# Regrouping the last rows of k and q for the first segment: through DRAM instead of by products with identity columns

## Chip, cores and metric

The kernel runs on one core of a Trainium2 chip. The metric is the device time of one execution in microseconds (us); the figure given for a kernel is the median of several runs. Beside it stands one profiled execution, whose trace shows every instruction of the engines: PE (TensorE, matrix products; PEld is its weight load), ACT (ScalarE), DVE (VectorE), POOL (GpSimd) and SP (SyncE, which here only issues DMAs).

## What is computed

Two layers, each an attention block with a memory and then a feed-forward block, on x of 2048 tokens by 640 in bf16:

```
x = x + A(layernorm(x)); x = x + B(layernorm(x))      # and the same once more
A:  q, k, v = x@wq, x@wk, x@wv           # 32 heads of width 20, 4 segments of 512 tokens
    for s in range(4):
        p     = softmax(q_s k_s^T * scale + causal mask)
        o_s   = g * (phi(q_s) M) / (phi(q_s) z) + (1 - g) * p v_s
        M, z += phi(k_s)^T v_s, sum(phi(k_s))          # phi(t) = t + 1 if t > 0 else exp(t)
    return o @ wo
B:  relu(x@w1) @ w2                                    # inner width 1728
```

## The kernel before

**Tiling.** Tokens go in 8 segment passes (2 layers `a` by 4 segments `s`), each of 4 tiles of 128 tokens. Per pass: layer norm (`ln1`), projections to k and q (`proj_kq`, products on L972) and to v (`proj_v`, L1017), the regrouping of k and q (`relay`), scores with exp and mask (`scores`, L1324, L1338, L1314), their product with v (`apply`, L1406), the memory's write and read (`mem_write`, L1187; `mem_read`, L1274), the output projection (L1598), and the feed-forward block (`ffn`, L1664 and L1696).

**The layout of k and q.** PE works on four heads at once, one in each 32-partition quarter. A head is 20 wide. The projection therefore gives 5 chunks `c` of 128 columns; in each quarter the rows 0 to 19 are one whole head and the rows 20 to 31 are 12 columns of the heads that are left over. So heads of the groups `g` = 0 to 4 can be used where they are (`kqA`), and the groups 5, 6, 7 lie scattered in the last 12 rows of the quarters of all five chunks. `relay` gathers them into `kqL` [128, 2, 3, 512]: k and q, three groups `m`, 20 rows in each quarter. There is one `kqL` buffer for all passes.

**Two ways to gather.** For the passes in `RELAY_PE`, which is pass 0 only, `relay_pe` (L1097 and on) does it on PE: DVE clears 128x896 elements of hT (L1104) and copies columns of the identity into it (7 copies, L1108), seven selection matrices; PE multiplies them with `kqA`, 7 products for k and 7 for q (L1130), and DVE or ACT moves the six results from PSUM to `kqL` (L1113, L1114). For the other passes `relay_dma` (L1054 and on) has SP issue four DMAs that write the leftover rows to a DRAM buffer `kq_scr` (L1067), one for each quarter, and four that read them back in the new grouping (L1080); read `r` waits for write `r`, and the first read waits for the `kqL` buffer. The reads fill 20 of the 32 rows of a quarter.

**Who needs kqL.** The scores of groups 5, 6, 7 (the second half of each pass's score rounds), the second half of the memory's write (a transposition by DMA, `ktok<-kqL`, L1169) and of its read (L1240, L1242).

**The order of work.** Nothing is ordered by hand. Each function is a stream of operations; a planner (`Sched`) simulates the engines with assumed costs and takes at each point the operation that can start first, ties by a due time. The due times are a packed table (`TABLE`), one entry for each operation. The planner's result is one fixed list of instructions for each engine, and every engine works its list in order. A wait for a semaphore at the head of a list therefore holds everything behind it on that engine. Where the planner foresees that PE is idle it puts products of the identity with itself there (L787), which nobody reads.

**Score rounds.** A pass has 4 pairs of head groups with 5 rounds each, 160 rounds in all; they are counted from 0 here. A round is one group of row-packed products (L1324) into four PSUM banks, X and Y of two banks each, and two exps of 1024 columns on ACT (L1335, L1338) that empty X and Y. There is only one X and one Y, so a round cannot begin before both exps of the round before are done.

Of the kernel before, what the change touches and what calls it, by code (L numbers as in the profile page):

```python
# [13 lines left out]
T = 2048  # L14
D = 640
# [399 lines left out]
c-n1R36PxCaqj<`nSW+>X7)a`yV_lyD+wJ)!srA^2nC57bA%g&v6En%!-WHJ2vANLTqGpeByk+u3Ak)0#*T>-n+lXU48g`6!2*dJBH0MtD<to-  # L415
+TH1V{rzwL9f50WXa3{8e%<~0_`2T=dh;YFS4mky*`@usUMx*gkOq7o))skR*N7(>8PRUZOG&<}H)2e$#Bu^=TqHj32IPNq0p4DOQ7xD|q#bzo
F}!J(Zuz!eg83JUYDoflTaUxsm3WuKT~X#@-
ZEUT2F)MpB8*&txv@mxXbS!pOBQe2<pZ6CcMEWx$C_nXj=39fH&q(tDP4`H%P}X1cLAvXP6zQFgL7Zz<LL^_4e>V{)Q*L0S-
hPMDp!NsoII$1Bv;7iF}7FE(Y10SB*=m8J$je)Vdg^oXD}m>=~!bSzT0F}7s@73+JrY{&}e}^ROjF-i&aC&RhC5<-
75#6xdE<Qz^5<osnJ}5F%cy_1<%*uNf#&|(q_nYw(QVRJwaa5UdlWNJMxlF1y`%V>lV2cn*7{>IdZuS%Bh&Y60}#!DmfF{x)2<%m*eCN{C`}Im  # L420
-F!KVm#X{)9}3zqff{4`53=I&Vdd#fci4I6!TWgXQf9@mYH%Rba^i%I8~NnPnUsGFXo*p*JJEC(D+GGkwx!s2DjtdggF`P&U#4k)Yxy-
Y$XfJ`3`p?gMBGLqB7((OPNsHAy4K8jd&W#I@zub(47wnV`w~!(Nn?SpnL}FuLFff>6BJJ&+|Kns|t98MnL^U*hruBgF-Xrbz(nk--
>us#P}w>?UhF$K^`O4Q~$GZH3hop!MG4}t7>~U4!do@{yithU~U7nGY_`jiE&dfvJclS;O{J0ZxK2?Pj0|$<F^3Gro$SF9NmP~m*Z&$94S1)$F
<o*1r!V5FvOS;Pks!KXp@~f4?c3dJgjHSZF&y&<WAiz-_r}_e9T@ZKhSBQ`m8R;+BfPK<xz}Z0~?qFKYd!~$}DJe8FU$dzS*{iRTe;>F>Sp;cI
z$j4NY{rM+ZRb=ekj@)9=fePUy#nM)h<0*R)8VR04e4E`^{Q;?Con0F;dO%Q_!-8MmwB>SOmj-
eujl&G1Oecb?}v+9BTr<kELkeb61&0-q$aJU2EO7sx?I3e~{zQg-Vk<92H&?^@-
ES{!)~mgv*QsyY*&UdoS2I0e$%T?F0}Sra;8y0+P6vzryvapc!s)u{QY&Q$%Bj#0Pg6~xT?`33xsz{*YLywkI-
P=wdm`^b&0*I3R`Ojb!g%aZKMkb0>mdl83BW`!mL$4A5~i&szaGbGnpzDX#SQ)!G+i8@K<+DzO1gd_V_jkpKC<K81})iB)+ua5s3$C*@ble!C>
mH2gYg1VVr9T#EBg@4p8*!ZlYQG24)Vwl>7UpFsKIr6CK(5(~Jt(Uw@WUS50lU~KyqvvF8!~gfB;G`JfxR}@bw4JMzQp@w5zH@alcq!-
pQQi{3X0vsc<~a}Xj*=x;_crm8_$c2=#@?@&r=v0-vgP_6O5}}G->qpgpq_#{E`y_dz+|43Be9M=RvJ}{_2!FJ{a4)t-  # L430
3@Dn(KW`qi2Mee5jv{&F5%{gR*4O&I;Iv|%z7Sot3=3)9{CJXFY|~38ek(e4^FgQ<1D6piA5;l;Sr69Hp~nDPxHLD-
Q1^U(RpVJH628$ABNy4N;O`;C#rsGLjkSiTD_+(=F~KtaFI{-=zS>KWf6;OUTfK}s>9Bj6Rk&_mv@mjgzq=YFZ6ExDbYjXg-Kk=xcxAlS~iO%$
!ig?PmIw;JU^GYIOF2v1htUt_@KN>3k>SwU&K|j={{#DwXIWC%lJhnT@nMcN7-
(eM#f2Lb06{LpiY0uK2FBYth@`Ks@earHabd~l(Ok1axtyqY(+KkM8D3eeV0YNRJz)Zj;Ue98OStt9Yd~~Ej2p|MHekPkU>5Ad8^~uG;U~SLNl
q%ReD3jT@75e*$ICB6WLvnb05%4X@{N2R@;D)F9F{V>K^bsKr6R34Rt?<wGQhH?BAQZ0%&2qynrViz+!(1tsB1mIV^Wn6TQxnFX+WirbvDu7m(
9`({BJ-
{7nB&p3pAfr04W`ptZMvE?VS8JxTr^IHFnpO#cMDd=WNsJy7Zea+UrI5Xr@w>`XykgRYBM?Jn7>kAsiXFzRKwS$`t$;QkR^3FPm~GvN3ZJozLj
P3SS0m4}QOd=CQI+yG>GraqyMK|?2k*3-HQX!Z?YohsJZ1wAy$m2$6MEvtbsmH|)g#Iqda-
347Pk#7Q#&zI*h_I{m>t9_by`cL(AVC!C>vcJ%4Py_hTNC}yKJJvd^H_NXyki@3fK$~~ye*Kl)4m<L(-
vjbr`X%URv24?KfgHvWffi#g{$2l+sPr_@zDXX?-Jn0N>rlnKp&dE`bk+*Xp9UOQhNb4@AN5MevQ>`<ZXDK-sBfE^XZ@8_t2bkA1NQD?u(6jk@  # L440
z=NXT=@$0)($=kpw%h+p}k|BhrJ5yVm>^ENZ2ELb*E0jPM#0c`k;Oal01Q`;{{c{O>f8DFMtilq3a#c`7YFHuj~7I1gk#`JzanuUoN)iIY!t#E
DSphdw2tJ`8TL0M(IbFK+37unWgf5)Eu3_RTi}#ghed}eFX;Vf~Gy}{{rrphuvwDSM(I<X^SQ?D?=pbgT`ZOaqJ+q;De_SRmqF`kbVOGqsR-
>G5Q)vFbCRu6?*>z_{P)Nt0(mtVA%lDSnc)-
<S>6P;kpm_`yJ>Z03JS1*2?4hvK|5wJ_xQo;Ho^Tkq1C&CUoax#$h1iS9A%auY!x0bqIS?1P=k8EX9oJ*nz{a6GIptQP?i*k%w&l&#<!}=_jG3
0j%gjjyyE+0yr=`58*BQIir=|kM6Y!BMSu9gBa2WZM4f}m@|xhvnV?c`6+`Oa|V383I7XOA6R5*g9ok_TXPw>ErUjc@iSNtSq0I8+Gr|9l_5<t
Yo2D==apI6lrbWU=Zo+;?B($$%TY0&&&K<z*8~YI@@KJcuR_iRGCWjp88L7<EO4khNORij@Ki5FhoQqg0Vs`Y*3HehsApsHE>4bs|G-
7qnArOa%zTBlkHzZ9eeTeHmnrsWk=~o+fv2fitC9|A4H<-xKI3p*m}Y(7;k+8E2^}Ju>yU*ZuLvv8f@hyi^ifJPaey7MXx#1O4%6IVk-
7vgw5qIumC^xN_Ct&u0c>K2nuUZen`G14VF~8M#N8pDn*A3U!EKeS6zR=16qhBI^-
!<9L5a%DJ*Jh|W&T=5EWl6WpouFO<w6}E@uc0w_);BKNos}3yMXtTHC^bCQO;qZz|}e)>}xM1_^~(FWoG{)$i0R-
BbTEi?m$$BA+ssAu1DDk66+#94eBtGC+~P!x7K8>k!0=2VLU&T#dEc0eVveX*HQXelfUdRy&<6@rGSTeE1b=E%;Y1Q<?ghl`M;`@n#&@BZ&l;H  # L450
s+klC#dW&18C%%jn9u}=WQd#+>-
hSR)v}j?&N?|6UVlEUXDL3<#s5LXq}ve*=YflzV~yk@MBJ#td(0*R#Ns^UC=;LhuC~jHS;97=YX$EO)ct#i=rL<mU$)@=y|^pT{#QvqX5NbUU!
-j<p-
%1tVr*xeXhQaF06I98bj*e~g2!oy7qg&;Cibxk)MuIXi230Tpcm_}l;wxueL14hLSV}r<7UozmT9cWew}p+R^jTcAP>DX%BQObv9n)?=G)~$tk
6!K<!P6O*cO4t2EPw9rpdmlX<(3uZYm>BVwr){)*|qEv0s#9;Uh<?ZH&h;?aVlthlrO)PB9u4%q+-
xen0r>m#3={Y0bj(3Z5T_nA<4d(u=@v8~(a5^J@o3by&o^#Q&=Qr1zwE{b(Q?pn*K)8zi4!!oBTJ9=!fBR=<h&){R<;b-U$R-
K<}xr*+5z@Hri;ty1fL?M2SE$XK9fM(ib8Cn%sjZ1AloRRlr`Q)wIMJBBWkn&0$s3|2nVudtW3QrnzI7C0l%{VY&-
t(dXe#`~ReGcx!IYF0d^&Ge59$C^bovO=)_YKNTVH-
K(IHi6$f?LSL9NcK6R=M|A*XMx7AfkGF8!@H1UU(z4x1+<m_M#c9Ca>#VCd}%iQhVGNwfM2&k+eh@bz)@>~VNOAYP4dT;au4!uH*H}Bvfo<pc^
2{iebT@0{_y1BcK^@)Z~51Gd*l;CKKIr9qJ=ZIsr3tABjTOQoYgKZE{4CRH&Mq~7qd;?9Am<#J=6YS4W0evV40@xOW9YPDdtICuF^O8ujE=|>_  # L460
8<^Iq5n5%nu~7jtKs08DJyp(Qh(uHL#j7EoQjevE1UtcsiGIx6uklfWflzhj`nIOkx@2Y*uuC!_06Md5gK0p@1T6FviSVnf*qPv8=0P+W4&eFZ
S%<fk0kjW?9TNHUkA$;I}cXAp?&L=qY9&OR;xL@z%z65^s3yhBshj3p><}SnDvbRRiPi!=N+8b$t4un*e$?-
cH0=I}NbjW}e;Fj2KtbL9Yvu?Oge#w~_tPHq0zypPS%|y_nqt4tm+wEfP26sPPur=;e7rPz2(ze(_v6fjTxVcHq8@=Uue*l6*$K2Cc0{)GRWlM
D*nzM6?*y&~DUBqwMFlV{D115F4a%=nl~9X1308?TA)jRbRiHiTNAg*#-QKYDnKJu&Z$yW$XkG3lY}??rV<T8O!PHD0hH<L_3>GezV-6vss-Qh
OD@1-lFS4%-
+bD(*PO+;Ac#&*Jn{;rMHgsTE$LJW~H6L9QNZ`XgtQ>G*FB1E+&#R>#E2Vkg*LjTQDY1`w7$2mGfxPru7o@O+Y^g<xWUz@n|~MGW}X6vgoh|*t
P&UOW>~oE8Oe4u7*t(%bdd{;G+uSRvD|6WGn1?9I<_nnhfPlZz^NT9Q<2%eY0o#n?cMy38RmZ2fXF5*e=krdbd}K-
Y{aoLh#qfPW?4NuZ=uO$suNR%BXx>PnKWm74jeQPl$PM4`rCs5;U5D@AWxE7BUJ==x(j`O;pVmTd>mG8r1b}B3j)95yuPO@9Xr|`j53vuOfE&b
$v9?#g*VAozKTTj~T&Z&(}*aTTs^nwEgL3oS5vuCa7+*Us|Jkh4;}eYJD%d_Bk)@_N_?KQZB_}7P~9t`93d0`&C`yR*mFSu-
1Z;vpJQ1viEPX|1D&&qSJgtq!96LkHbn<=_OIZV%RaLx;(~#T8GEp?L|!=JFa}zcA@JCCEdmr&^pO8ssoHLwGL_Iuvp|!k(~_MN#D5ou39*{Lv  # L470
K58*m)14#ZGAYQN2@+1?G7XGB?UIsB8aLAA?P7VQp=5zN_CsKG}o2HS&4AL4JafwmVx<Wqv{L0L3?T1`z&;9s<VOg?PJ1P139^_utWLVJVM#1-
SuhUFX?ZW}{4aMb!UamJ+JAQxTOe@+xu@yySJc95G^Czp}r=D&QSh<{bF!Hh4i1HnSD?Q?Rzx%AJz*Oxxifji73A<;7|Reld#udJpe^3+uldRA
vzC`KVv7b6RUb-FyYIQGxmXQu<(4uEp9DK#!++0dY!(Q36)uXP6rTFGsK4j<GTRuk&*3z79fW8+)=Ju^MQ^vkBDTSNa9Un?~?x5qo549wJo|4V
w|yy10|gkaxQD^Sq~(-0oL9*=+(h(-
2>~u<t#LUu9w!>lt?<F6~BC9w3?;LpGWZxwEn!JJAT5eXh3dl;`y%AdXewD2D#quyO~hUpp7+#tL?7d<68nAWu7V{Q;2p9_XzXE4AYDu+C)XZy
M-LWwh?V%nr~R2N$+iZFtj4i8~QN$9c9iTa0Qq#zx>F2U!L%s}18K%4;W#W1!MSls}5~+A+QZ@5gaH40+l)s$UXsYJ>-m06ke=?xM^l#T0O1^-
DW6)5CL6<Hszqm0f@aj6H(bG={yfTxsXD@9XhcZz(t&(LVah0%X#6)wt*Zr3UiX4O-@b-
IzZMZw81;T3FwAkf&xm9hB2xV*{XXu{i@BHR0V__DhP4D;<>jfW8d$w_oo#U=g5+IW?kX7>^~!ge<h)Lmv*A`2tp;7H5We#vM}+A?+~7GpUH@n
n%=X>~2OStCm|BhcZMPhNF_-6g1G5^Q@5aq!TdKST-HkF?dWr=j3r`8tr1{d|OwOQ(Iv~r;zVhHpz4BwMN8^&9YMq>;NQuwKKA2xOM=I?B%&$>
^cK6=_Qp~(#x^_UxuhZCRc`*CiokP5P0(gwUdz|y{a7;dL5BPi8CsUk9n?Y&jNOd^3Ipd^U92qdCra{<2ni%H!tLFh3rw)PR%3crHDBwPr7AB)  # L480
GVLoIHFcl<d~6?+A>cGLU#rkledV~nlFiVa+EpXnY&p*!L8lEm6BOG?taeU=GgU(lHUd7nNefr#Vk>L)^+#IE<>W%fEJaN1bh3`bl`SAVEhOi>
JNE_A4!7YlGE^zk;|lO;+P`2GUS@2-
6h&7lX`(Du|Uk9fgi@qd#3Y!>?#%TEW?#6ls3mZ>o5e2WC1lE(#mp9x5@c@34YQ=jTNaq`|fu;VMuMaF6R0rR`eNav52@~`><aVyPrnPSa9#GX
WB%HyL1lqm!Z#PDNCMvJAtT~Alg>M(8pb6TX7X*!f8ajpQlYtXmZAB=&p?C&E!2sR0-
H$Ni41mZfDX{^X_!5KzlOo^G?%A57D|8_FJNWZ><M#mOR9|sl@l+)g5}5WDe}m26huHd$*+>t%@8{JAv5^&$Zt-
*x8f$=XS)s8Xme@4)N6EAw37t?y%O*=6;PV@44R-yw03qyFMQ|bpfR6p^Qz?`(kzsRPAJ-lfNozk-LFrJJ_!c5nC?<IxQmeSeN?-M8-C`-
Aj6oWjyJ}tXI4a))y7A-&*v`_Mx{?1!Q=_H+jyb{GEbFysBDdd<z)I522bl0t}{_SmfMP10}}jPV7sW$kp~Tg9>{F-rH}4CUi(!-
7hyHqT4L^Pr7}+!^5`Pa@PY6-KmwG)^74YV8_WYQ|vIIYJ#(^&lMbnJttUeMJe4PdpmY!`@F7nIQI^(c7kU)KSAorpXWM^3H2-^jQ^ouJ{;>-
+zvG3Io#LhotSp}{PY~Z_Pd4p^YxjoXX?u(QgTn%r|7>m?IvC?dC&5G(jN?%Q<9$G2gG)hJk?H-GxXkoeW#>0w=Q;LdRG1qvdXI=^=8+--
hxVW62E7OO!NFs`n$7{{gQs_<T-rR{j#D%b`0gA-O%aMPRMgIq=vVCr>5Ee2aARbqy  # L490
"""


# [1300 lines left out]
```

## Time and profile before

| what | value |
|---|---|
| median of 7 runs | 565.67 us (565.45 to 566.09) |
| the profiled execution, its own time | 565.72 us |
| its span, first to last instruction | 564.0 us |
| PE busy | 556.1 us, 99% of the span, 5197 products |
| ACT busy, DVE busy, POOL busy | 426.5, 420.1, 207.8 us |
| L1130, the products of `relay_pe` | x14, first at 19.1 us, last at 33.2 us |
| L1067 and L1080, the DMAs of `relay_dma` | 28 each, 120 KB each, first at 57.5 and 70.9 us |
| granted TensorE clock | 1.0 throughout |

The profile is one execution. Busy times are sums of instruction durations; PE's are pipelined and overlap, so that two products in a row begin closer together than one of them lasts. For the pace of PE one reads the starts in the timeline. "Idle before" names what ended the wait of an engine.

### The profile page before, as it was taken

Reading aid. Unit: us, or ns where it says so; the run is one execution under the profiler, and the core shown is the slowest. Engines: PE = TensorE matmul, PEld = TensorE weight load, DVE = VectorE, ACT = ScalarE, POOL = GpSimd, SP = SyncE. Lnnn points to the kernel's source line nnn. Section 1 sums busy time; section 2 is a strip of 40 time slices with the busy share of each in tenths; the row PEclk is TensorE's granted clock in tenths of the full one; section 3 lists DMA queues with packets and bytes.
Section 4 is the critical chain, followed back from the end, with each engine's and each line's share of the span. In section 5 each row is a group of like instructions: output and inputs, shape, how many; then the busy total and the mean of one; then the engine's idle time right before and its main releaser. Section 6 shows DMA issues by size and latency. Waiting matters only on the chain.

```text
span 564.0 us, 12683 instructions
## 1 busy us (share of the span) xinstructions
PE 556.1 (99%) x5197; PEld 297.1 (53%) x5197; DVE 420.1 (74%) x1037; ACT 426.5 (76%) x523; POOL 207.8 (37%) x323
## 2 busy tenths in 40 slices
PE   8999999999999999999999999999999999999998
PEld 5444545445654445545456454564545653755655
DVE  6798989998998766877789966899678775643202
ACT  4899999998898988689898977978889677123140
POOL 3555445643444332453334433144333334002000
PEclk9999999999999999999999999999999999999999
DMA  6447697845534446465255533573315531431201
GB/s 221 132 125 142 140 155 157 223 105 104 95 69 61 66 80 79 65 110 98 53 59 106 87 65 59 78 110 68 65 20 94 101 75 20 90 71 31 63 1 48
DMA packets 127410, 50.63 MB, mean 90 GB/s; under 512 B 112152, under 2 KB 125400, under 8 KB 127352
## 3 DMA queue, kind: packets, MB, share of 16 engines
q1 hardware_dynamic: 125224, 42.03, 41.5%
q0 software_dynamic: 1552, 7.29, 4.5%
q8 instruction: 41, 0.67, 0.5%
q10 hardware_dynamic: 576, 0.50, 0.3%
q14 instruction: 17, 0.14, 0.1%
HBM read 15.16 MB, written 7.37 MB: 40 GB/s over the span
## 4 chain that ended last, share of the span: by engine, by line
PE 86%; DVE 8%; DMA 3%; ACT 2%; POOL 1%; issue 0%
PE ps L1664 20%; PE ps L1696 19%; PE ps L972 14%; PE ps L1324 8%; PE ps L1017 8%; PE ps L1598 6%; PE ps L1406 6%; DMA otok<-oraw 1%; PE ps L1274 1%; DVE stats L887 1%; ACT PT L1338 1%; DVE stats L888 1%; PE ps L1187 1%; DVE x_sb L1540 1%; DMA xnT<-xn_tok 1%; PE ps L1676 1%
## 5 line engine op out<-in xcount | busy, mean ns | idle before, releaser
L1338 ACT ACTIVATE PT<-ps 128x1024 bf16<-128x1024 f32 x256 | 248.2, 1024 | 39.4 <-PE ps L1324 38.3
L1314 POOL TENSOR_SCALAR_AFFINE_SELECT PT<-PT 128x512 bf16<-128x512 bf16 x256 | 169.5, 679 | 247.5 <-ACT PT L1338 205.8
L1696 PE MATMUL ps<-wb,hT 128*128 128x320 bf16 x896 | 136.0, 299 | 0.0
L1664 PE MATMUL ps<-xnT,wb 128*128 128x512 bf16 x520 | 126.3, 380 | 0.1
L1540 DVE TENSOR_TENSOR x_sb<-x_sb,ps 128x320 bf16<-128x320 bf16 x128 | 60.8, 478 | 70.4 <-PE ps L1696 52.3
L1696 PEld LDWEIGHTS ps<-wb,hT 128*128 128x128 bf16 x896 | 83.5, 98 | 37.7 <-issue 6.0
L1634 ACT ACTIVATE hT<-ps 128x512 bf16<-128x512 f32 (+1 forms) x66 | 38.3, 580 | 54.1 <-PE ps L1664 53.1
L1664 PEld LDWEIGHTS ps<-xnT,wb 128*128 128x128 bf16 x520 | 47.9, 98 | 55.8 <-issue 6.4
L1335 ACT ACTIVATE PT<-ps 128x1024 bf16<-128x1024 f32 x64 | 62.1, 1023 | 10.8 <-PE ps L1324 10.8
L1017 PE MATMUL ps<-wv_r,xnT 128*128 128x320 bf16 x320 | 58.8, 300 | 0.0
L972 PE MATMUL ps<-xnT,wq_p 128*128 128x512 bf16 x200 | 55.5, 380 | 0.0
L972 PE MATMUL ps<-xnT,wk_p 128*128 128x512 bf16 x200 | 54.9, 380 | 0.0
L1598 PE MATMUL ps<-wo_r,oT 128*128 128x320 bf16 x280 | 50.5, 299 | 0.0
L1633 DVE TENSOR_SCALAR hT<-ps 128x512 bf16<-128x512 f32 (+1 forms) x46 | 31.0, 674 | 15.8 <-PE ps L1664 15.5
L1406 PE MATMUL ps<-PT,va 128*32 128x128 bf16 (+3 forms) x896 | 40.7, 302 | 1.2 <-POOL PT L1314 1.2
L1017 PEld LDWEIGHTS ps<-wv_r,xnT 128*128 128x128 bf16 x320 | 29.6, 98 | 18.3 <-issue 2.1
L959 DVE CAST kq<-ps 128x512 bf16<-128x512 f32 x41 | 28.1, 686 | 12.0 <-PE ps L972 11.6
L1324 PE MATMUL ps<-kq 20*128 20x512 bf16 (+3 forms) x560 | 35.3, 301 | 0.0
L1598 PEld LDWEIGHTS ps<-wo_r,oT 128*128 128x128 bf16 x280 | 26.6, 98 | 15.2 <-issue 2.3
L902 DVE TENSOR_SCALAR xn_tok<-x_sb,mv,rstd 128x640 bf16<-128x640 bf16 x64 | 30.5, 494 | 3.5 <-POOL rstd L898 1.7
L1406 PEld LDWEIGHTS ps<-PT,va 128*32 128x32 bf16 x896 | 19.2, 96 | 23.1 <-issue 10.2
L887 DVE BATCH_NORM_STATS2 stats<-x_sb 128x6 f32<-128x320 bf16 x64 | 29.5, 466 | 2.0 <-DMA x_sb<-in_A_x_dram 1.7
(116 smaller groups left out, 622.5 us busy)
## 6 DMA issues: line engine op xcount, KB each, us to landing
kq_scr<-kq SPq DMA_DIRECT2D x28, 120.0 KB
kqL<-kq_scr SPq DMA_DIRECT2D x28, 120.0 KB
out_dram<-x_sb SPq DMA_DIRECT2D x15, 160.0 KB, 1.8
wb<-in_B_w_dram POOLq DMA_DIRECT2D x5, 432.0 KB, 4.2
x_sb<-in_A_x_dram POOLq DMA_DIRECT2D x3, 640.0 KB, 4.9
wb<-in_B_w_dram POOLq DMA_DIRECT2D x2, 640.0 KB, 7.1
kq_away<-hT SPq DMA_DIRECT2D x5, 256.0 KB, 2.6
kq<-kq_away SPq DMA_DIRECT2D x5, 256.0 KB, 3.4
```

Source lines behind the costliest of these rows:

```text
L972: fn = lambda e, bank, k=k, w_p=w_p, c=c: e.matmul(bank, w_p[:, k, c * 128:(c + 1) * 128], xnT[:, k_, :, k, :], start=(k == 0), stop=(k == ...
L1017: fn = lambda e, bank, k=k, i=i, hf=hf: e.matmul(bank[:, 0:320], xnT[:, k_, i, k, :], wv_r[:, k, hf * 320:(hf + 1) * 320], start=(k == 0), ...
L1314: tm = yield pool(590.0, lambda e: e.affine_select(out=reg, in_=reg, pattern=[[0, 4], [1, 128]], compare_op=ALU.is_ge, fill=0.0, base=0, c ...
L1324: fns.append((lambda e, x=x, j=j, hh=hh, N=N, o=o: e.matmul(ps[:, hh, o:o + N], kq(b, gg[x], 0)[32 * hh:32 * hh + DH, 128 * j:128 * j + 12 ...
L1335: fn = lambda e: e.activation(PT[:, :, 2 * k:2 * k + 2, 1024:1280], bs.ap.rearrange("p h (x t) -> p x h t", x=2), ACT.Exp, scale=SCALE)
L1338: fn = lambda e: e.activation(PT[:, items[0], 2 * k:2 * k + 2, c0:c0 + 512], bs.ap, ACT.Exp, scale=SCALE)
L1406: return [(lambda e, hh=hh, j=j: e.matmul(bank[32 * hh:32 * hh + 32, 128 * j:L], v_flat[b][:, (j * H + 8 * hh + g) * E1:(j * H + 8 * hh + ...
L1540: ta = yield dve(320, 1, lambda e: e.tensor_tensor(xa, xa, bk.ap[:, 0:320], ALU.add), [tk], early=HOT)
L1598: fn = lambda e, bank, k=k, hf=hf, o=ot.ap: e.matmul(bank[:, 0:320], o[:, k, :], wo_r[:, k, hf * 320:(hf + 1) * 320], start=(k == 0), stop ...
L1634: lambda e: e.activation(d, bk.ap[:, 0:n], ACT.Relu), [tk] + hs[0].old + (hs[1].old if dc >= NSTG // L else []))
L1664: fn = lambda e, bank, k=k, dc=dc: e.matmul(bank, w1_r[:, k, dc * 128:(dc + 1) * 128], xnT[:, k_, :, k, :], start=(k == 0), stop=(k == FC ...
L1696: fn = lambda e, bank, dc=dc, q=q, h=h, hf=hf: e.matmul(bank[:, 0:320], h, w2_r[:, q, hf * 320:(hf + 1) * 320], start=(dc == 0), stop=(dc ...
```

## The change

`RELAY_PE` becomes empty, so pass 0 is gathered by `relay_dma` as well. Since the DMAs leave 12 rows of each quarter of `kqL` unwritten, and no product writes them any more, POOL clears the whole of `kqL` once, early in its list, and the first read of pass 0 waits for that. The table of due times is another one, so the order of many operations on every engine differs.

```diff
 TABLE = """
-c-n1R36PxCaqj<`nSW+>X7)a`yV_lyD+wJ)!srA^2nC57bA%g&v6En%!-WHJ2vANLTqGpeByk+u3Ak)0#*T>-n+lXU48g`6!2*dJBH0MtD<to-
...
+c-m!JdyJgbbwBree>1Z)`}Xd7cfG6)#>Rl{0Jgynn1okAZ6FW`G=hpWP0}>2(tx5?Ak>6bm0Bfj8bK0OQKhyj=}UsN5mgaM)$&i(K-
...
 """
...
         HALVES = ()
-        RELAY_PE = (0,)
+        RELAY_PE = ()
...
                 th = yield pool(150, lambda e: e.memset(nhalf[:], -0.5))
+                tz = yield pool(3300, lambda e: e.memset(kqL[:], 0.0))
+                S.set("zkq", v=[tz])
                 S.set("nhalf", v=[th])
...
                 for c in range(5):
                     KQA[b][c].drop(*wr)
+                zs = []
+                if (a, s) == (0, 0):
+                    zs = yield Need("zkq")
                 rd = []
...
                     if sl is None:
-                        tk, sl = yield dma("sp", scr_sem[r], 122880, lambda e, s_, f=f: f(e), [wr[r]], [KQL],
+                        tk, sl = yield dma("sp", scr_sem[r], 122880, lambda e, s_, f=f: f(e), [wr[r]] + zs, [KQL],
                                            users=3 + (s > 0) + (s < NSEG - 1), rate=80.0)
```

## The prediction

> **What bounds the kernel now.** I read the page's busy times first, then the waits of PE, then PE's timeline around the products that go, then SP's and POOL's timelines for what takes their place.
>
> ```profile
> PE 556.1 (99%) x5197; PEld 297.1 (53%) x5197; DVE 420.1 (74%) x1037; ACT 426.5 (76%) x523; POOL 207.8 (37%) x323
> ...
> DVE  6798989998998766877789966899678775643202
> ACT  4899999998898988689898977978889677123140
> ```
> PE has no slack anywhere; but in slices 2 to 8 (14 to 113 us), where pass 0 lies, ACT and DVE are almost as full. From 20 to 110 us they are busy 87.1 and 84.3 of 90 us. A gain on PE there can be taken back by ACT.
>
> ```profile
> PE ps L828 <- DVE ktok L825: 1.2, 1, 1.2
> PE ps L1406 <- POOL PT L1314: 1.2, 1, 1.2
> PE ps L853 <- DVE xn_tok L902: 0.9, 1, 0.9
> PE ps L1324 <- ACT PT L1335: 0.9, 1, 0.9
> PE ps L1130 <- DVE kqL L1113: 0.2, 1, 0.2
> ```
> All waits of PE that the trace shows as idle are a few single ones. Two belong to the start, one is of the relay itself. So the span is PE's list at PE's pace, plus single stalls.
>
> ```profile
> 21.33 0.30 PE L1017 MATMUL ps<-wv_r,xnT 128*128 128x320 bf16 x1
> 21.56 0.40 PE L1324 MATMUL ps<-wb 20*128 20x384 bf16 x8
> ...
> 27.74 0.81 PE L1130 MATMUL ps<-wb,hT 128*128 128x512 bf16 x3
> 28.39 0.38 PE L972 MATMUL ps<-xnT,wq_p 128*128 128x512 bf16 x1
> ...
> 80.80 0.39 PE L1324 MATMUL ps<-kq 20*128 20x512 bf16 x4
> ...
> 83.22 0.40 PE L1324 MATMUL ps<-kq 20*128 20x384 bf16 x8
> ```
> Three paces, all from starts. Three L1130 take 28.39 - 27.74 = 0.65 us, 0.217 each (the 0.38 of one is mostly pipeline). A 320-column product takes 0.133 (ten L1017 in 1.36 elsewhere), but 0.23 pass before the row-packed L1324: changing the packing costs 0.10. And 83.22 - 80.80 = 2.42 us is the closest that two score rounds come: one round's two exps (1.94) and the way to them must be over first.
>
> **What the Trainium skill says.** "TensorE: Matmul & The Clock Gate", Back-to-back issue gap, gives N/2.4 + 2.5 ns for a lone product, 216 ns at 512 columns, and 131 ns sustained; the trace agrees with the first (217) and not with the second. "DMA: Bandwidth & Descriptors", Anatomy of one DMA, puts about 2 us of fixed cost on each, mostly the receipt of the write; the trace shows no landing for the relay's DMAs, only that a read could be issued 3.5 us after the first write (below). "SBUF — State Buffer", Who interferes with whom: GpSimd shares a port pair with DVE, and a DVE instruction with one input outside the two-port modes does not contend; no wait in the trace speaks against it. "GPSIMD Engine Reference", 3.1, gives 1.03 to 1.8 cycles an element at 1.2 GHz for simple bodies; the maskg clear below is at 1.1.
>
> **The change part by part.**
>
> *The 14 products go.* 14 x 0.217 = 3.0 us of PE, all on the path, since PE never waits for long. From the lists as built I count 389 changes of packing before and 394 after: +5 x 0.10 = +0.5. Identity products (L787) fall from 25 to 21; they fill idle time and count nothing. All other products are the same in number. Net -2.5 us.
>
> *Six evacuations, one clear and seven copies go.* L1113 and L1114 pace 0.6 us each: 3.0 us of DVE, 0.6 of ACT. They are not on PE's path themselves. What PE may gain is in rounds 4 to 6 (27 to 35 us): comparing starts with pace, PE loses 0.16, 0.37 and 0.30 us there, 0.2 of it named above. I take -0.5; bounds 0 (another evacuation takes the place) and -0.8. DVE's clear and copies (L1104, L1108) end at 2.4 us, and DVE then waits until 4.1 for x: worth nothing.
>
> *The start.* In the new DVE list the first xn_tok stands two instructions earlier, ahead of an aggregate and a statistic, so it can begin at 6.5 instead of 7.0. The fourth tile's is bound by POOL (rstd ends 9.7) as before, and PE is full only from there. I take -0.1, bounds -0.4 and 0.
>
> *POOL clears kqL, 128x3072, before its first rstd.*
> ```profile
> 0.79 0.20 POOL L782 MEMSET ident<- 128x128 bf16 x1 [0.29 <-POOLq L1779]
> ...
> 1.61 0.10 POOL L792 MEMSET nhalf<- 128x4 f32 x1
> 5.50 0.55 POOL L898 TENSOR_TENSOR rstd<-lnU,nhalf 128x1 f32<-128x1 f32 x1 [3.78 <-DVE lnU L894]
> ...
> 20.82 0.68 POOL L806 MEMSET maskg<- 128x672 bf16 x1
> ```
> (0.68 - 0.20) / (672 - 128) = 0.88 ns a column, so 3072 take 0.20 + 2944 x 0.88 ns = 2.8 us, from 1.7 to 4.5 us. The cover is POOL's wait of 3.78 us for DVE's lnU, ended at 5.4: 0.9 us to spare. Cost 0. At the skill's slow end (3072 x 1.8 / 1.2 GHz = 4.6 us, an estimate from that page) it would end at 6.3 and hold rstd, and with it all that follows, by 0.9 us. The lower bound is 0; nothing gets earlier by a clear.
>
> *Eight more DMAs on SP.*
> ```profile
> 42.20 8.49 SPq L873 DMA_TRANSPOSE xnT<-xn_tok  x3
> 50.73 1.36 SPq L1161 DMA_TRANSPOSE ktok<-wb  x1
> 52.13 1.31 SPq L1533 DMA_TRANSPOSE otok<-oraw  x1
> ...
> 54.86 1.65 SPq L1169 DMA_TRANSPOSE ktok<-kqL  x1
> ...
> 357.39 3.47 SPq L1067 DMA_DIRECT2D kq_scr<-kq  x4
> 360.91 4.44 SPq L1080 DMA_DIRECT2D kqL<-kq_scr  x4
> ```
> At 357 us four writes and four reads follow each other directly: 8.0 us from first to last issue. In the new list of SP the order is: ktok (first half), four writes, read 0, xnT x2 of pass 2, read 1, otok of pair 0, reads 2 and 3, ktok, xnT x2, otok of pair 1, ktok<-kqL. The writes need chunk 4 of k and q. By pace its last product ends near 27.2, so the writes are out from about 28 to 31, read 0 near 32. The xn_tok of pass 2 stands at 16.9 us of busy sum in the new DVE list after its statistics begin (at 2.0, when x arrives near 18.7: issued by 13.8, median landing 4.9), so near 34; otok of pair 0 follows the second apply, near 38, so 39.5; reads 2 and 3 near 41; landed by 46 if I allow 5 us. PE first needs kqL in round 12. In the list that is 47.8 us of pace, plus some 5 (PE's lag on pace in the trace is 5.2 at round 12): 52.6. Cover 6 us; cost 0. Behind ktok<-kqL waits ACT's exp L1177 after round 16 (near 60); otok of pair 1 goes at about 52, ktok<-kqL at 53.5, as before (54.9), so no change. The DMA share from 28 to 46 us is 0.4 to 0.8, so there is room for 960 KB more.
>
> *The other order.* From the same pace I laid out the starts of the 160 rounds in both lists. From round 36 to 51 the spacing is the same to 0.01 us, and the last 300 products stand in the same order; in between they differ little. But in the new list some rounds stand closer than 2.42: from 12 to 13 there is 1.96 us of PE work (with 0.03 that each round loses to pace), 17 to 18 2.20, 21 to 22 2.28, 23 to 24 2.35, 2 to 3 2.29, 30 to 31 1.53, 31 to 32 1.81, 52 to 53 1.72. PE must stand still for the difference: 0.46 + 0.22 + 0.14 + 0.07 + 0.13 + 0.89 + 0.61 + 0.70 = 3.2 us. In the old list only 52 to 53 (1.04) and 23 to 24 do: 1.4, and the trace has it: PE loses 1.42 at round 53. So +1.8; bounds +1.0 (if work lost elsewhere in PE has already spread the rounds) and +2.5 (with the ACT operations that stand between some of these rounds).
>
> *The rest.* The stall of 1.2 us at L1406 <- POOL (232 us; lnU and rstd stand before three masks) has one mask ahead of rstd in the new list; 0, bounds -0.6 and +0.5. Small new waits in a new order I can't see: 0, bounds -0.5 and +1.5.
>
> Sum: -2.5 - 0.5 - 0.1 + 1.8 = -1.3 us. The profiled execution took 565.72 (span 564.0 and 1.7 around it), so 564.4; the median of the runs is 0.05 below it, which doesn't matter here.
>
> **Rivals.**
>
> *A: the tight rounds cost nothing more, PE's gain is whole.* 565.7 - 2.5 - 0.5 - 0.1 = 562.6. For it: PE lags pace in many places and the rounds spread. Against: ACT has 97% busy there, and round 53 shows that the 2.42 holds.
>
> *B: a new wait eats what is left.* ACT is the real bound of passes 0 to 2, so that PE's 3 us become idle: 565.7. For it: the 3.2 us of shortfall and ACT's fullness. Against: by the trace's durations ACT's new list is also about 3 us shorter between rounds 0 and 36 (fewer evacuations on it).
>
> *C, on the other side: SP's list delivers kqL late.* Reads 1 to 3 stand behind transpositions that wait for layer norm and apply. If pass 2's xn_tok come as late as before (second xnT near 45.1 + 1.3), reads 2 and 3 go at 49, and with the slowest landing of a ktok transposition in this trace, 8.2 us, in a stretch where the DMA share is 0.96 to 1.0, kqL is there at 57.2. PE stands at round 12 from 52.6 for 4.6 us with ACT and DVE behind it: 564.4 + 4.6 = 569.0. It turns my gain to a loss from a landing at 53.9 on, and is slower by over 0.2% from 55.0 on. Against: 9 us of earlier readiness by my count.
>
> *D: POOL's clear at its slow end*, +0.9: 565.3.
>
> **How the numbers follow.** My forecast 564.4 (own range 563.2 to 565.7): 0.55. A 0.17, B 0.12, C 0.11, D 0.05. Below A I go 0.1 for the start's bound, and up to where C begins to be half: low 562.5, high 566.8. About 0.2% (1.1 us, 564.5 to 566.8) is what a measurement of this kernel can tell from no change. Of the forecast some 0.36 of its 0.55 lies below 564.5, with A 0.53 faster; of B, D and the rest of the forecast 0.34 same; C and part of B 0.13 slower.
>
> **What would show it.** L1130, L1113, L1114 gone; 32 of L1067 and of L1080, the first L1080 near 32 us and the fourth near 41; PE's first wait for ACT's exp at rounds 13, 31 and 32 with 0.4 to 0.9 us each (about 2 us more of "L1324 <- ACT" in PE's waits), and less of it at 53; POOL's clear of 2.8 us ended before 5.4; first score on kqL near 52.6 with no wait for a DMA. If PE waits for a DMA at L1324, C holds. If the sum of PE's waits doesn't grow, A does. If waits grow by 3 us or more in rounds 0 to 36, B does.

## The result, and the profile after

The changed kernel takes 564.3 us (median of 13 runs, 563.95 to 564.88) where the kernel before takes 565.82 us (31 runs beside it): ratio 0.9973, 95% interval 0.9966 to 0.998, so 1.1 to 1.9 us less. The forecast was 564.4. The profiled span went from 564.0 to 562.2 us. All ratios below are to runs of the kernel before on the same chip; they can differ by up to 0.0006 from the quotient of the two medians.

The line numbers after are 2 to 7 lower than before (L1324 is now L1322, L1406 is L1404, L972 is L967, L1017 is L1012). First the page of after, busy times and two rows of the slices:

```profile
PE 554.5 (99%) x5179; PEld 295.8 (53%) x5179; DVE 414.7 (74%) x1031; ACT 422.1 (75%) x516; POOL 208.2 (37%) x323
...
DVE  6799979997999778866689866998678865724202
ACT  4899989998899877688998878879788867023140
```

PE is busy for 1.6 us less, DVE for 5.4, ACT for 4.4, and PE is still at 99%. Then the waits of PE after (what waits, for what: us in total, times, longest):

```profile
PE ps L1322 <- ACT PT L1336: 1.8, 3, 0.8
PE ps L823 <- DVE ktok L820: 1.2, 1, 1.2
PE ps L1012 <- DVE o_sb L1261: 0.5, 1, 0.5
PE ps L967 <- DVE kq L954: 0.5, 1, 0.5
PE ps L1694 <- DVE x_sb L1538: 0.4, 1, 0.4
```

The waits for exps have grown from 1.1 to 1.8 us (about 2 us more were forecast), three waits for PSUM banks that DVE frees (`o_sb`, `kq`, `x_sb`) are new, and the 1.2 us of L1406 <- POOL are gone. PE's timeline after at rounds 30 to 32:

```profile
100.08 0.40 PE L1322 MATMUL ps<-kq 20*128 20x512 bf16 x4
100.41 1.25 PE L967 MATMUL ps<-xnT,wq_p 128*128 128x512 bf16 x5
102.50 0.40 PE L1322 MATMUL ps<-kq 20*128 20x384 bf16 x8 [0.84 <-ACT PT L1336]
...
104.93 0.29 PE L1322 MATMUL ps<-kq 20*128 20x256 bf16 x4 [0.36 <-ACT PT L1336]
```

102.50 - 100.08 is 2.42 us again. POOL's clear and SP's DMAs, each from that engine's timeline after:

```profile
1.65 2.66 POOL L786 MEMSET kqL<- 128x3072 bf16 x1
5.15 0.55 POOL L893 TENSOR_TENSOR rstd<-lnU,nhalf 128x1 f32<-128x1 f32 x1 [0.85 <-DVE lnU L889]
```
```profile
29.28 1.60 SPq L1062 DMA_DIRECT2D kq_scr<-wb  x4
33.38 0.27 SPq L1078 DMA_DIRECT2D kqL<-kq_scr  x1
...
41.80 0.92 SPq L1078 DMA_DIRECT2D kqL<-kq_scr  x2
...
54.03 1.44 SPq L1167 DMA_TRANSPOSE ktok<-kqL  x1
```

The clear ends with 0.85 us to spare, the reads are out by 42.7 us, and the first round on `kqL` (round 12) starts at 53.34 us with no wait for a DMA.

**Where the time went.** I laid both lists out at the prediction's paces, without any spacing, and compared them with the starts of the rounds. What a stretch takes beyond pace is lost there:

| rounds | lost before, us | lost after, us | difference |
|---|---|---|---|
| 0 to 3 | 0.21 | 1.01 | +0.80 (round 1: 0.72) |
| 3 to 6 | 0.74 | 0.00 | -0.74 |
| 12 to 19 | 0.09 | 1.25 | +1.16 (rounds 13, 18: 0.67, 0.54) |
| 29 to 36 | 0.45 | 1.76 | +1.31 (rounds 31, 32: 0.90, 0.62) |
| 51 to 60 | 1.85 | 1.28 | -0.57 (round 53: 1.39 to 0.91) |
| 76 to 78 | 1.29 | 0.01 | -1.28 (round 77) |
| all others | 0.85 | 0.91 | +0.06 |
| all 160 | 5.48 | 6.22 | +0.74 |

The work at pace falls by 2.5 us (549.9 to 547.4), so 2.5 - 0.74 = 1.8 us are left, which is the gain of the span. But look where: round 36 starts at 115.41 before and at 115.43 after. Up to there the list has 2.6 us less work and PE has stood still for all of it. The gain appears at rounds 51 to 60 and at round 77, far from the change.

### The profile page after: what moved, and what is told of

It reads as the page before. It is cut to its first block, busy times and chain, and to the rows that moved or that the text cites. A ratio compares the mean times of both kernels' runs of the same rounds, so it can differ in the third digit from the quotient of the medians.

```text
span 562.2 us, 12649 instructions
## 1 busy us (share of the span) xinstructions
PE 554.5 (99%) x5179; PEld 295.8 (53%) x5179; DVE 414.7 (74%) x1031; ACT 422.1 (75%) x516; POOL 208.2 (37%) x323
## 4 chain that ended last, share of the span: by engine, by line
PE 91%; ACT 6%; DVE 2%; issue 1%
PE ps L1694 21%; PE ps L1662 21%; PE ps L967 14%; PE ps L1322 9%; PE ps L1012 8%; PE ps L1596 7%; PE ps L1404 7%; ACT PT L1336 3%; PE ps L1185 1%; PE ps L1272 1%; PE ps L823 1%; PE ps L1674 1%; ACT PT L1333 1%; ACT etmp L1175 0%; PE ps L848 0%
## 5 line engine op out<-in xcount | busy, mean ns | idle before, releaser
L1538 DVE TENSOR_TENSOR x_sb<-x_sb,ps 128x320 bf16<-128x320 bf16 x128 | 60.8, 479 | 71.2 <-PE ps L1694 45.5
L1632 ACT ACTIVATE hT<-ps 128x512 bf16<-128x512 f32 (+1 forms) x63 | 36.9, 586 | 51.4 <-PE ps L1662 50.7
L1012 PE MATMUL ps<-wv_r,xnT 128*128 128x320 bf16 x320 | 57.0, 300 | 0.5 <-DVE o_sb L1261 0.5
L967 PE MATMUL ps<-xnT,wk_p 128*128 128x512 bf16 x200 | 53.8, 380 | 0.5 <-DVE kq L954 0.5
L967 PE MATMUL ps<-xnT,wq_p 128*128 128x512 bf16 x200 | 54.0, 380 | 0.1
L1631 DVE TENSOR_SCALAR hT<-ps 128x512 bf16<-128x512 f32 (+1 forms) x49 | 32.5, 664 | 15.5 <-PE ps L1662 15.0
L1404 PE MATMUL ps<-PT,va 128*32 128x128 bf16 (+3 forms) x896 | 40.7, 302 | 0.0
L1012 PEld LDWEIGHTS ps<-wv_r,xnT 128*128 128x128 bf16 x320 | 29.4, 98 | 18.8 <-issue 2.9
L954 DVE CAST kq<-ps 128x512 bf16<-128x512 f32 x43 | 29.5, 687 | 12.8 <-PE ps L967 12.5
L1322 PE MATMUL ps<-kq 20*128 20x512 bf16 (+3 forms) x560 | 35.3, 301 | 1.4 <-ACT PT L1336 1.2
L1404 PEld LDWEIGHTS ps<-PT,va 128*32 128x32 bf16 x896 | 19.0, 96 | 21.2 <-issue 9.3
```

The costliest lines, as they stand in the source:

```text
L967: fn = lambda e, bank, k=k, w_p=w_p, c=c: e.matmul(bank, w_p[:, k, c * 128:(c + 1) * 128], xnT[:, k_, :, k, :], start=(k == 0), stop=(k == ...
L1012: fn = lambda e, bank, k=k, i=i, hf=hf: e.matmul(bank[:, 0:320], xnT[:, k_, i, k, :], wv_r[:, k, hf * 320:(hf + 1) * 320], start=(k == 0), ...
L1322: fns.append((lambda e, x=x, j=j, hh=hh, N=N, o=o: e.matmul(ps[:, hh, o:o + N], kq(b, gg[x], 0)[32 * hh:32 * hh + DH, 128 * j:128 * j + 12 ...
L1404: return [(lambda e, hh=hh, j=j: e.matmul(bank[32 * hh:32 * hh + 32, 128 * j:L], v_flat[b][:, (j * H + 8 * hh + g) * E1:(j * H + 8 * hh + ...
L1538: ta = yield dve(320, 1, lambda e: e.tensor_tensor(xa, xa, bk.ap[:, 0:320], ALU.add), [tk], early=HOT)
L1632: lambda e: e.activation(d, bk.ap[:, 0:n], ACT.Relu), [tk] + hs[0].old + (hs[1].old if dc >= NSTG // L else []))
```

## The experiments

Two theories at the start. **T (order, spacing):** what PE no longer does becomes standing time between rounds that are too close, and the gain comes from stalls that the new order happens not to have. **R (own place):** the gain is the regrouping's own work, the other differences are noise of the order.

**1. The 14 products at a sixteenth of their width, old order.**

```diff
-  bank, sel[:, i], kqA[b][:, n, c, :], start=(z == 0), stop=(z == k - 1))
+  bank[:, 0:32], sel[:, i], kqA[b][:, n, c, 0:32], start=(z == 0), stop=(z == k - 1))
```

> The kernel before, its 14 identity-column products (L1130) cut from 512 to 32 columns; the regrouped k and q of pass 0 get stale PSUM values in the other columns, everything else and all orders stay. This prices PE's work alone, in the old order. PE saves about 14 x (0.217 - 0.017) = 2.8 us. Theory T (spacing): a round can't start less than 2.42 us after the one before, and the products stood between rounds that have little other work; by pace rounds 2, 4, 5 and 6 then come 0.21 + 0.57 + 0.95 + 0.31 = 2.0 us too close, so only 0.7 is left: 565.1. Rival R (own place): PE's work is PE's time, the whole 2.6 to 2.8 us come off: 563.1.

565.14 us against 565.63, ratio 0.9997 (0.9988 to 1.0005): nothing that can be told from zero. Beyond pace, rounds 2, 4, 5 and 6 lose 0.98, 0.58, 0.96 and 0.64 us where T had 0.21, 0.57, 0.95 and 0.31; round 36 comes at 114.74, 0.67 us earlier than before. PE's timeline of this run:

```profile
24.34 0.40 PE L1324 MATMUL ps<-wb 20*128 20x256 bf16 x8 [0.85 <-ACT PT L1338]
```

R falls for PE's work: 2.8 us of it taken out of this place are worth 0.2 us, 0.7 at most by the interval (0.9 in the one profiled execution). The six evacuations are still in this run; nothing here takes them out alone.

**2. The DMA regrouping under the old due times.** The new table is replaced by one made of the old one's entries; the code is the changed kernel's.

> The change without its new table of due times: DMA regrouping of pass 0 and the clear, but the due times of the kernel before for every operation that both kernels have (the eight DMAs take the place in the ranking that they have after). Theory T (spacing): what the change is worth is decided by the order. In this list rounds come closer than 2.42 us by 10.0 us in all (rounds 4, 5, 15 to 17, 24, 31 to 34, 51 to 58), 8.5 more than before, with 2.8 us less of other PE time: 565.8 + 5.7 = 571.5, range 569.5 to 573. Rival R (own place): the regrouping itself is worth the 1.5 us and the order is incidental: 564.3, within 1 us.

579.28 us, ratio 1.0244 (1.0228 to 1.0261): 13.6 us slower. T has the direction, its spacing only 5.7 of it. The largest single loss, 5.15 us at round 17, is another mechanism. Views of this run: SP's issue with its time to landing, the timelines of ACT, DVE and PE, and the granted clock in 40 slices of 14.5 us.

```profile
ktok<-kqL SPq DMA_TRANSPOSE x1, 11.3
```
```profile
64.27 1.06 ACT L1166 ACTIVATE etmp<-ktok 128x1024 bf16<-128x1024 bf16 x1 [1.46 <-DMA ktok<-kqL]
```
```profile
65.36 0.49 DVE L1167 TENSOR_SCALAR ktok<-ktok 128x1024 bf16<-128x1024 bf16 x1 [1.14 <-ACT etmp L1166]
```
```profile
66.66 2.29 PE L958 MATMUL ps<-xnT,wk_p 128*128 128x512 bf16 x5 [3.40 <-DVE rmem L1251]
```
```profile
PEclk9999799999999999999999999999999999999999
```

Read from top to bottom: the transposition of `kqL` lands 11.3 us after its issue (5.7 before, 5.3 after), ACT's list stands for it, DVE's stands for ACT, and PE's for DVE, whose `rmem` stands behind that `ktok`. PE had been idle since 63.3 us, so its wait is the longest, 3.40 us. That is rival C with another DMA. The same code with the table of the change has none of it. The other 1.7 us of round 17's loss are no wait: in this run the granted clock (1.0 in the other profiles) is 0.5 from 64.4 to 71.2 us, and products of 512 columns start 0.427 us apart instead of 0.217. From 187.3 to 190.7 us it is 0.5 again. By an estimate, from the time that PE is busy in the two stretches (4.6 and about 3.4 us, half of it lost), the clock accounts for some 4 of the 13.6 us, which neither theory had.

**3. Two masks ahead of lnU and rstd, in the kernel before.** Only four entries of POOL's list change places (and the semaphore counts that others wait for); the lines show the two orders, not the code.

```diff
 POOL, from 228 us:
-  lnU, rstd, mask, mask
+  mask, mask, lnU, rstd
```

> The kernel before with two masks moved ahead of lnU and rstd in POOL's list at 228 us, nothing else (regrouping still on PE, all other lists the same). Theory T (order): this is the stall of 1.2 us (PE's wait at L1406 for POOL) that the change lost only by its other order: 565.8 - 1.2 = 564.6. Rival R: the time found there goes into the next wait, for rstd's xn_tok comes 1.3 us later, and nothing is gained: 565.8.

564.38 us against 565.63, ratio 0.9976 (0.9969 to 0.9982). POOL's and PE's timelines, first of the kernel before, then of this run:

```profile
228.84 0.69 POOL L894 TENSOR_SCALAR lnU<-mv 128x4 f32<-128x4 f32 x1 [3.23 <-DVE mv L889]
229.61 1.04 POOL L898 TENSOR_TENSOR rstd<-lnU,nhalf 128x4 f32<-128x4 f32 x1
230.62 2.31 POOL L1314 TENSOR_SCALAR_AFFINE_SELECT PT<-PT 128x512 bf16<-128x512 bf16 x3
...
232.31 0.73 PE L1406 MATMUL ps<-PT,va 128*32 128x512 bf16 x16 [1.21 <-POOL PT L1314]
```
```profile
227.71 1.22 POOL L1314 TENSOR_SCALAR_AFFINE_SELECT PT<-PT 128x512 bf16<-128x512 bf16 x2 [2.09 <-ACT PT L1338]
229.07 0.69 POOL L894 TENSOR_SCALAR lnU<-mv 128x4 f32<-128x4 f32 x1
...
231.12 0.73 PE L1406 MATMUL ps<-PT,va 128*32 128x512 bf16 x16
```

Round 77 loses 0.01 instead of 1.29, and little else moves. This is as much as the whole change brings (0.9973), with the old regrouping in place. T holds here: by the table above 1.28 of the change's 1.8 us are this stall, and it hangs on the order of four POOL instructions. The reverse, the old order of these four in the changed kernel, was not run.

**4. Short exps in after.**

```diff
+  if 5 * m + u in (12, 17, 30, 31, 52):
+      fn = lambda e: e.activation(PT[:, items[0], 2 * k:2 * k + 2, c0:c0 + 32], bs.ap[:, :, 0:32], ACT.Exp, scale=SCALE)
```

> The kernel after with the exps of rounds 12, 17, 30, 31 and 52 cut from 1024 to 32 columns each (the other columns of these score blocks keep old values); orders stay. Rounds 13, 18, 31, 32 and 53, which follow them, lose 0.70, 0.57, 0.92, 0.65 and 0.93 us in the profile of after. Theory T (spacing by the exps): at least rounds 31 and 32, where PE's wait is for ACT's exp, lose nothing now, -1.5 us: 562.8; if the exps are behind 13, 18 and 53 too, -3.7: 560.6. Rival R: PE is held there by PSUM banks that wait for DVE's and ACT's evacuations, the exps are only the last to come; then the waits move to the next release and the gain is under 0.5 us: 564.0.

565.94 us, ratio 1.0008 (1.0 to 1.0016): 2 us slower than the changed kernel, outside both expectations. Rounds 13 and 18 lose what they lose in after (0.66, 0.54), so the exps were never behind those two. Round 31 loses nothing now, but 32, 33 and 36 lose 1.09, 0.68 and 0.58. PE's, DVE's and POOL's timelines of this run, and DVE's of after at the same place:

```profile
102.95 0.45 PE L848 MATMUL ps<-ident,xn_tok 128*128 128x128 bf16 x5 [0.78 <-DVE o_sb L1261]
```
```profile
103.73 1.12 DVE L1178 TENSOR_TENSOR ktok<-ktok,etmp 128x1024 bf16<-128x1024 bf16 x1
```
```profile
100.33 3.98 POOL L1312 TENSOR_SCALAR_AFFINE_SELECT PT<-PT 128x512 bf16<-128x512 bf16 x5
```
```profile
103.55 0.68 DVE L1178 TENSOR_TENSOR ktok<-ktok,etmp 128x1024 bf16<-128x1024 bf16 x1
```

PE now waits at the next place, for a PSUM bank that DVE empties. And DVE itself got slower: L1178 takes 1.12 us where its 24 instances in after take 0.67 to 0.73. POOL's masks, released earlier, run beside it (five in a row, 0.80 us each instead of 0.62), and what differs is which begins first: here a mask began 0.19 us before L1178, while in after masks begin during 11 of the 24, and those keep 0.67 to 0.69. The Trainium skill, "SBUF — State Buffer", Who interferes with whom, says that a DVE instruction with two SBUF inputs contends with a GpSimd instruction that reads SBUF; the 1.12 and the 0.80 us agree. Something like it is seen at round 53: beside four masks in a row an `xn_tok` takes 0.92 us instead of 0.43, and PE waits 0.90 us for the `x_sb` behind it instead of 0.42. About half of the 2 us is lost there, at rounds 51 to 60; a wait of 0.67 us for a transposition of `xn_tok` is among it, and what delayed that was not followed. T's spacing by the exps is thus only one of several limits that come within a few tenths of each other.

**5. The clear as bytes.**

```diff
-  tz = yield pool(3300, lambda e: e.memset(kqL[:], 0.0))
+  tz = yield pool(3300, lambda e: e.memset(kqL[:].bitcast(dt.uint8), 0))
```

> The kernel after with POOL's clear of kqL written as bytes: the same zeros, twice the elements. If a clear's time goes by elements it takes 5.3 us instead of 2.66 and ends near 7.0, and the first rstd, which has 0.85 us to spare, starts 1.8 us late. Theory T (the first rstd is on the path): everything after it shifts, 564.3 + 1.8 = 566.1. Rival: the start is bound by something else too (the weights' arrival, DVE's statistics of the four tiles), and less than 0.5 us comes through: 564.3 to 564.8. If the clear goes by bytes, its 2.66 us don't change and the run says nothing on the cover.

The clear takes 5.21 us and ends at 6.83; the first rstd starts 1.68 us later than in after, round 0 0.92 us later (21.05), and round 159 0.91 us later (474.95): nothing of it is absorbed in between. 565.04 us, ratio 0.9996 (0.9988 to 1.0004), where after has 0.9973. Between the two expectations: about half of the delay comes through the four tiles' chain, and all of that stays.

**6 and 9. The casts of ones on POOL.** In after three casts of ones (L799) stand on ACT ahead of the first exp; round 1 waits for it. In run 6 they go to POOL where their turn comes, in run 9 behind POOL's clear of `maskg` and its DMA for x. The edit of run 6, shortened:

```diff
-  ("act", act_ns(128, False), 125.0, one(lambda e, o=o, i=i: e.activation(o, i, ACT.Copy)))
+  y = act(128, lambda e, o=o, i=i: e.tensor_copy(o, i), [ta], psum=False); y.put = "pool"
```

> The kernel after with the three casts of ones (L799) put on POOL, which is idle then, instead of ACT, where they stand 1.65 us long ahead of the first exp; all other lists the same. Theory T: round 1 loses nothing more (0.72 us in the profile of after), later rounds stay as they are: 563.6. Rival (waits only move): ACT and DVE are full until 110 us, the rounds come to the same later limits and less than 0.2 us is left: 564.2.

> The kernel after with the three casts of ones (L799) on POOL again, but behind its clear of maskg and its DMA for x, which they held up in the run before; all other lists the same. Theory: round 1's 0.72 us go, and since the shift of the clear came through whole, so does this: 564.3 - 0.7 = 563.6. Rival (waits only move, as they did in the run before): round 2 takes it, 564.2 or more.

567.04 us, ratio 1.0024 (1.0012 to 1.0036), and 565.36 us, ratio 0.9996 (0.9987 to 1.0006): both slower than after. Round 1's loss is gone in both, but round 2 loses 2.34 and 1.40 us. In run 6 the clear of `maskg` stands behind the casts and DVE waits 2.34 us for it. In run 9 nothing of that is left; DVE's timeline and POOL's beside it:

```profile
19.06 1.93 DVE L842 CAST maskg<-gt 20x160 bf16<-20x160 f32 x1
```
```profile
18.99 0.77 POOL L830 CAST wb<-gt 128x128 bf16<-128x128 f32 x1 [0.83 <-ACT gt L824]
19.35 1.54 POOL L830 CAST va<-gt 128x128 bf16<-128x128 f32 x2
```

A DVE cast that takes 0.23 us in after takes 1.93: it ends when POOL's three casts have ended. Layer norm's statistics stand behind it, and the transposes of xn_tok (L881) wait 1.2 us. So the stall of round 1 is real, and POOL isn't the place to put its cause.

**7 and 8. Rounds moved in PE's list.** Work and the other lists unchanged. The lines give the moves, not the code: (round, instructions that now come first).

```diff
 run 7, kernel before, with POOL's swap of run 3:
+  (53, 10), (54, 18), (55, 3), (56, 16)
 run 8, kernel after:
+  (31, 14), (32, 11), (33, 24), (34, 20), (35, 5), (36, 17), (37, 8), (38, 3), (39, 16), (53, 5), (54, 3), (55, 1), (57, 3)
```

> The kernel before, regrouping on PE kept, with two edits of the lists and none of the work: the two masks ahead of lnU and rstd at 228 us (as in the run above), and the score rounds 53 to 56 moved behind 10, 18, 3 and 16 of the products that followed them, so that rounds are 2.4 us apart where 53 stood 1.04 behind 52. Theory T (order): round 53's 1.39 us go but for 0.5 at round 57, which is now 1.9 behind 56: 565.7 - 1.25 - 0.9 = 563.5, faster than the change. Rival (slots): the products that now come first wait for PSUM banks that DVE frees no sooner, and only the 1.25 of POOL's list are gained: 564.4.

> The kernel after with the score rounds 31 to 39 and 53 to 57 moved behind some of the products that followed them (14, 11, 24, 20, 5, 17, 8, 3, 16 and 5, 3, 1, 3 instructions), work and other lists the same. By pace the shortfall against 2.42 us falls from 3.4 to 2.0 us. Theory T (spacing): 564.3 - 1.5 = 562.8. Rival (slots): from 98 to 108 us DVE has no idle time, and the products that come first need PSUM banks that only DVE's list frees; nothing is gained at 31 to 39, some 0.5 at 53: 563.8 to 564.3.

565.51 us, ratio 1.0001 (0.9993 to 1.0009), by the ratios 1.4 us worse than run 3 alone; and 569.04 us, ratio 1.0067 (1.0054 to 1.008). Round 53 still loses 1.40 us in run 7: its products wait 0.78 us for DVE's `x_sb` (a PSUM bank) and the move only puts two later rounds behind. In run 8 the moved transposes wait 1.1 us for `o_sb` and the projection 1.4 us for `xnT`; rounds 29 to 36 lose 4.31 us instead of 1.76. The rival has the mechanism in both runs, but both lose more than it expected (564.4 and 563.8 to 564.3): none of these moves finds PE ready work to take instead.

**10. Reads 2 and 3 of the regrouping three places later on SP.**

> The kernel after with the reads 2 and 3 of pass 0's regrouping moved three places later on SP, behind the first ktok transposition and two of xnT: issued near 51.7 instead of 41.8 us; all else the same. PE first needs kqL at 53.3. This measures the landing that the trace doesn't show, and the price of the cover. With my 5 us from issue to landing kqL is there near 57, PE stands in round 12 for some 3.7 us and all behind it shifts: 568.0. With a landing of 2.5 us: 54.5, 1.2 us: 565.5. With the slowest of a transposition, 8.2 to 11 us: 60 to 63, 571 or more. If nothing is lost, round 12 doesn't wait for these reads at all and the cover was never needed: 564.3.

They are issued from 52.02 to 52.93 us. PE's timeline of this run at round 12:

```profile
55.90 0.29 PE L1354 MATMUL ps<-wb 20*128 20x256 bf16 x4 [2.18 <-DMA kqL<-kq_scr]
```

So the last read lands some 3.0 us after the end of its issue, 2.25 us are lost, and all of it stays: 566.95 us, ratio 1.0019 (1.0012 to 1.0027), 2.6 us above after. In after the last read goes at 42.7, would land near 46 by this, and is needed at 53.3: 7 us of cover.

**11 and 12. DVE relieved near 100 us, then DVE and the exps of rounds 30 and 31.**

```diff
+  cut = slice(0, 32 if (a, s, h, g0) == (0, 1, 0, 2) else 1024)   # ktok, L1176 and L1178
+  j1 = 1 if n == 9 else 2 * NJ                                    # otok, L1479
```

> The kernel after with three DVE instructions near 100 us cut: one pair of ktok (L1176, L1178) from 1024 to 32 columns and one product of otok (L1479) to an eighth, so that parts of ktok and otok keep unfinished values; 1.7 us less of DVE there, nothing else. New theory (two full engines): rounds 31 and 32 are held by ACT's exps and by DVE's evacuations at about the same time; with DVE alone relieved the exps still hold them: 564.3, rounds 31 and 32 lose over 1.0 of their 1.5 us. Rival (DVE alone is the bound, the exps only look so): 562.8.

> As the run before, and the exps of rounds 30 and 31 cut from 1024 to 32 columns as well. New theory (two full engines): only now rounds 31 and 32 lose nothing, 1.5 us come off, and they stay off behind it: 562.8. Rival (a third limit, or DVE slowed where POOL's masks come earlier, as with the short exps alone): the rounds behind take it back, 563.8 to 564.5.

564.48 us, ratio 0.998 (0.9974 to 0.9986), and 564.08 us, ratio 0.9972 (0.9961 to 0.9983): neither can be told from after. With DVE alone relieved rounds 31 and 32 lose 0.90 and 0.62 as before, as the new theory had it. With both, round 31 loses nothing and 32, 33 and 36 lose 0.36, 0.52 and 0.59; round 36 comes 0.2 us earlier than in run 11, not 1.5. PE waits for the next thing:

```profile
104.67 0.45 PE L848 MATMUL ps<-ident,xn_tok 128*128 128x128 bf16 x5 [0.45 <-DVE xnT L863]
```

So two limits are not enough to explain it either.

## Why the prediction was right, and where it was not

The total was right within 0.2 us (-1.5 for the -1.3 of the sum; -1.8 in the profiled span), but part of that closeness is luck. What it missed on one side, 1.28 us at round 77, is about what it missed on the other, 0.72 us at round 1 and 0.45 at the tight rounds. The places differ too: by its own terms some 0.6 us of the gain should have stood at round 36 (-3.1 and +2.5) and 0.7 at round 53; measured are none, 0.6 at rounds 51 to 60, and 1.3 at round 77.

- **The 14 products, -2.5.** Right as work: 2.5 us at pace. But I took all of it to lie on the path and charged the losses separately; run 1 shows that in the old order 2.8 us less of it shorten the run by 0.2 us, 0.7 at the most. (The pace of 320 columns is 1.36 / 10 = 0.136 us, not 0.133; it changes nothing here.)
- **The evacuations, rounds 4 to 6, -0.5.** They lose 0.74 us less: right, inside its bounds; that the missing evacuations are the cause was not tested alone.
- **The start, -0.1.** Round 0 comes 1.41 us later with 1.40 us more work before it: nothing gained, inside its bounds.
- **The clear.** 2.66 us for 2.8, 0.85 us to spare for 0.9, cost 0: right. Run 5 gives the price if the cover is gone: 0.9 us for 1.7 us of delay.
- **The eight DMAs.** Right, down to the order on SP; the landing that I allowed 5 us takes 3.0 (run 10). "No change" for ktok<-kqL was right for this order and is the thinnest part of the argument: run 2 has the same DMAs in a little different surroundings and PE stands 3.4 us for it.
- **The other order, +1.8.** The places were right: rounds 13, 18, 31, 32 and 53 lose 0.67, 0.54, 0.90, 0.62 and 0.91, together 3.6 where I had 2.9 for them, and 53 lost 1.39 before, so +2.25. The mechanism was too simple: at 13 and 18 PE waits for PSUM banks (`o_sb` and `kq`, 0.5 us each; run 4 leaves them as they are), at 53 for `x_sb` (0.4 us; with short exps it loses no less), and only at 31 and 32 are the exps the first of several limits.
- **The stall at L1406 <- POOL, 0 with bounds of -0.6 and +0.5.** The largest miss: all of it went, -1.28. I saw that one mask stands ahead of rstd in the new list and didn't follow which mask the apply waits for. Run 3 shows that in the old order it alone is worth as much as the whole change.
- **The rest, 0.** Round 1's 0.72 us were missed: I didn't look at what stands on ACT ahead of the first exp.

Of the rivals, A falls: the tight rounds cost what they seemed to. B describes the first 115 us exactly (all of PE's gain becomes idle) and misses what the order gives later; its cause, ACT alone, is not shown, for shorter exps didn't help. C didn't occur, but runs 2 and 10 show it real. D falls with the clear's 2.66 us.

Open: what holds rounds 12 to 36. Shown is that PE's order, the exps, three DVE instructions, and the exps with those each don't lift it. Whether a further PSUM bank would was not tried: the kernel uses all eight of its `ps`. No list edit tried is clearly faster than the changed kernel.

## What to carry to other kernels

Work taken out of a stretch where the other engines are nearly full (here ACT 97% and DVE 94% busy from 20 to 110 us) need not be time gained, even on the engine that is 99% busy: compare the time at which the stretch ends, not the waits that went away. When a change brings another order of everything, give each named stall of the old profile its own fate in the new list, however far from the change; in a kernel with fixed lists the order of four instructions (run 3) can weigh as much as the change. And a faster engine is no gift by itself: shorter exps released POOL's masks into DVE's way, and the run took 2 us more.

## What was not expected of the hardware

- A DVE cast of 20x160 takes 1.93 us instead of 0.23 beside three POOL casts in a row. The Trainium skill, "SBUF — State Buffer", Who interferes with whom, has a cast among the operations that can take the port pair shared with GpSimd when their operands allow it, and says that the one that comes second blocks; POOL's first cast begins 0.07 us before DVE's, which agrees. In my prediction I had leaned on its sentence on instructions with one input. Here the wait lasts through three POOL instructions, not one.
- A clear of the same bytes on POOL takes 5.21 us as uint8 against 2.66 as bf16: its time goes by elements.
- A transposition by DMA of the same size lands after 5.3, 5.7 or 11.3 us in three orders. What makes the difference was not isolated; in the slow case a load of weights issued between 52 and 56 us took 10.9 us too, against 4.9 in after.
- In run 2 the granted clock fell to 0.5 about 1.1 us after PE's last product had ended, inside the wait of 3.40 us, and stayed there for 6.8 us. The second fall, for 3.4 us, came without a wait over 0.9 us, when PE had been busy for 1.9 of the 4 us before it. Single waits of 2.2 us (runs 6 and 10) brought none.
